# Two halves to a block: pv and scores of a sparse-attention kernel in three blocks per chunk, not six

## The chip, the cores and the metric

The kernel runs on one core of a Trainium2 chip. The metric is the device time of one execution in microseconds (us). Three runs of the kernel before took 757.9, 758.04 and 759.26 us; the median is 758.04.

## What is computed

The input has 4 batches, 8 heads, 768 positions and 64 columns per head, all in 32-bit floats. A block-sparse attention is followed by a two-layer net with a squared relu:

```python
scores = scale * np.matmul(q, k.transpose(0, 1, 3, 2))
mask = np.abs(blk_i - blk_j) <= window            # blocks of 32, window 1
mask |= first and last block, as a query or as a key
mask[...] = True                                  # 3 sampled blocks per block of queries
scores = np.where(mask, scores, -1000000000.0)
attn = exp(scores - max); attn /= sum + 1e-09
x = (attn @ v)  as 3072 tokens x 512
h = np.maximum(x @ w_in, 0.0)                     # 512 x 2048
return h * h @ w_out                              # 2048 x 512
```

(Lines of the reference, shortened; `attn`, `x` and the mask's second line stand for several lines each.)

## The kernel before

**Tiles and chunks.** A batch has six tiles of 128 queries (four blocks of 32). Three tiles make a chunk of 384 tokens, so that there are 24 tiles in 8 chunks, and an even chunk begins a batch. A tile's work is done in two halves of four heads each (class `Half`). A block of 32 queries has 256 keys at its place: the first and the last block, three sampled and three of the window.

**The MoE of a chunk** (`moe`, `hidden`, `project`) is a loop over 16 slices f of the hidden layer. `turn` transposes the chunk's three tiles (xt, L773). Then for each f come `project(f - 2)`, nine matmuls into three accumulators (po, L826), and `hidden(f)`, twelve matmuls into one bank (ph, L788). To keep the precision, each operand is split into a high and a low part: ACT makes r and gh from ph (L792, L799), DVE makes gf (L804) and the casts wi and wo (L754), POOL makes the low parts gl (L806), wi and wo (L755). The results of a chunk are stored when the next one has begun.

**The attention of chunk c + 1 runs inside the MoE of chunk c.** The MoE's generators stop after every 3 or 4 matmuls; one such stop is a piece, 96 to a chunk, six to a slice f. `Stream.step` is called at each piece, first goes on with the units that have begun, then starts new ones, and each unit says by `yield n` how many pieces later it wants to go on. The engines take their instructions in the order in which they are written here. So the table `LAG`, `STEP` (16 pieces from one half to the next), `EARLY` and `G_AT` set the order on every engine.

**A half from the seventh tile on** (`MOVED`): scores `s` are 64 small matmuls from kn (the batch's keys, window) and KG (gathered keys) into two PSUM banks (L374). DVE takes maxima (L385) and subtracts them (L391), which frees the banks. ACT takes 16 exps of 32 rows each, which also move blocks (pm, L413). DVE turns pm into pT (L418). PE then makes pv, 64 small matmuls from pT and V (L459), and DVE divides (`norm`, L474 to L479). With the table's numbers pv of one half falls on the piece at which the scores of a later one begin: a block of pv and s, six per chunk. The first six tiles go another way (exps with a bias, transposes pt on PE).

**The first and last block of queries** of a batch see all keys. These are `Whole` units, one per pair of heads, four per batch, in even chunks: scores g (L546), maxima, exps into pg, 32 copies of 32 rows into pgm (L571, by ACT and POOL in turns), a transpose by DVE (L577), and pvg (L604), which needs vn, the batch's values in two halves. One buffer holds vn: its second half is loaded when pvg of the second pair has read the first.

**Buffers and loads.** Five PSUM banks are handed out in turn to ph, xt, s, g, pv and pvg; three more hold the accumulators po. V has one buffer for each half of the heads, KG has two tiles, kn one buffer per half. SP issues nearly all loads, in the written order: after pv of a half the V rows of the next tile (one or two window loads L304, a read of the sampled indices L231, twelve sampled loads L317); with the scores of a tile's second half q (L242) and the gathered keys of the tile after next (L276, twelve); at a batch's last tile kn, QG and vn of the next batch (L175, L170, L222). The KG slots for the first and last block of keys are copied from kn by ACT (`next_keys`, `static_keys`, L284), for tiles 0 and 1 of batches 1 to 3.

Of the kernel before, what the change touches and what calls it, by code (L numbers as in the profile page):

```python
# [10 lines left out]
F32 = mybir.dt.float32  # L11
# [61 lines left out]
LAG_1 = {**LAG, "v": 10, "x": 3, "t": 6, "v0": 5, "n": 0}  # L73
LAG_0 = {"s": 2, "x": 2, "t": 3, "c": 2, "v0": 2, "n": 2}

CUT_0 = (30, 5)
# [20 lines left out]
def tile_block_sparse_attention_moe(ctx: ExitStack, tc, kd, knd, qd, qgd, vd, vnd, samp, const, wcat, out):  # L97
# [182 lines left out]
    def static_keys(b, t, u, copy=nc.scalar.copy):  # L280

        src = st["kn", b, u][:, 0 : NBLK : NBLK - 1].rearrange("p i a c -> p i (a c)").unsqueeze(1)
        dst = st["kg", b, t][:, :, 0:2, 2 * u : 2 * u + 2].rearrange("p j i a c -> p j i (a c)")
        copy(dst, src.broadcast_to(list(dst.shape)))  # L284
# [39 lines left out]
    class Half:  # L324
# [8 lines left out]
        def run(self, bank, lag):  # L333

            self.scores()
            self.loads(0)
            yield lag["s"]
            self.maxima()
            if self.moved:
                yield lag["e"]  # L340
                yield from self.turn_blocks()
                yield lag["v"]
            else:
                yield lag["x"]
                self.exps()
                self.next_keys()
                yield lag["t"]
                pt = self.turn(bank)
                yield lag["c"]
                self.copies(pt)  # L350
                self.loads(1)
                yield lag["v0"]
            po = self.values(bank)
            if lag["n"] >= 0:
                yield lag["n"]
            self.norm(po)
            self.loads(2)
# [37 lines left out]
                    op=ALU.subtract,  # L395
                )

        def next_keys(self):

            b, t = order[min(self.k + self.u, len(order) - 1)]  # L400
            if b > 0 and t < 2:
                static_keys(b, t, 1 - self.u)

        def turn_blocks(self):


            x = self.p.rearrange("p h c a s -> p (h c) a s")
            p = rot.tile([P, NJ, 8, BLK], F32, tag="p", name=f"pm{self.name}", bufs=PBUFS)
            for j in range(NJ):
                if j == 2:  # L410
                    self.next_keys()
                for a in range(NJ):
                    nc.scalar.activation(  # L413
                        p[a * BLK : (a + 1) * BLK, j], x[j * BLK : (j + 1) * BLK, :, a], AF.Exp, scale=SCALE
                    )
                    yield 1
            self.pT = rot.tile([P, NJ, 4, 2, BLK], F32, tag="pT", name=f"pT{self.name}", bufs=2)
            nc.vector.transpose(self.pT.rearrange("p j h c q -> p (j h c q)"), p.rearrange("p j x s -> p (j x s)"))  # L418

        def exps(self):  # L420
            for e in range(2):
# [59 lines left out]
        def loads(self, step):  # L481
# [19 lines left out]
            if step == 2 and k not in range(1, UC) and n < len(order):  # L501
# [2 lines left out]
                load_window(n, self.u)  # L504
                load_sampled(n, self.u, nc.sync, SP)

    class Whole:


        n = (16 * BLK, 8 * BLK)  # L510

        def __init__(self, b, pr):
            self.b, self.pr = b, pr
            self.name = f"{b}_{pr}"

        def run(self, bank, lag):
            self.scores()
            yield lag["s"]
            self.maxima()
            yield lag["x"]  # L520
            self.exps()
            yield lag["t"]
            if self.b > 0:
                yield from self.move()
                yield lag["w0"]
                self.turn_blocks()
                yield lag["w"]
# [36 lines left out]
        def move(self):  # L564

            self.pm = rot.tile([P, NJ, NT, BLK], F32, tag="w", name=f"pgm{self.name}", bufs=WBUFS)
            x = self.p.rearrange("p (k a s) -> p k a s", k=NT, a=NJ)
            for g in range(NJ):
                for a in range(NJ):
                    copy = nc.scalar.copy if a % 2 else nc.gpsimd.tensor_copy  # L570
                    copy(self.pm[a * BLK : (a + 1) * BLK, g], x[g * BLK : (g + 1) * BLK, :, a])  # L571
                    if a % 2:
                        yield 0

        def turn_blocks(self):
            self.pT = rot.tile([P, S], F32, tag="pT", name=f"pTg{self.name}", bufs=2)
            nc.vector.transpose(self.pT.rearrange("p (k g q) -> p g k q", k=NT, g=NJ), self.pm)  # L577

        def turn(self, bank):
            pt = [bank(f"ptg{self.name}_{i}") for i in range(2)]  # L580
# [4 lines left out]
            return pt  # L585

        def copies(self, pt):
            self.pT = rot.tile([P, S], F32, tag="pT", name=f"pTg{self.name}", bufs=2)
            for i, n in enumerate(self.n):
                at = i * self.n[0]  # L590
                if i == 0:
                    nc.scalar.copy(self.pT[:, at : at + n], pt[i][:, :n])
                else:
                    nc.vector.tensor_copy(self.pT[:, at : at + n], pt[i][:, :n])

        def values(self, bank):
            b, pr = self.b, self.pr
            vn = st["vn", b, pr // 2]
            po = bank(f"pvg{self.name}")
            for kt in range(NT):  # L600
                a = kt * P
                for g in range(4):
                    h = pr % 2 * 2 + g % 2
                    nc.tensor.matmul(  # L604
                        po[g * BLK : (g + 1) * BLK, :VW],
                        self.pT[:, a + g * BLK : a + (g + 1) * BLK],
                        vn[:, kt, h * VW : (h + 1) * VW],
                        start=(kt == 0),
                        stop=(kt == NT - 1),
                    )  # L610
            return po
# [16 lines left out]

    def units(c):

        halves = [Half(b, t, u) for b, t in order[c * UC : (c + 1) * UC] for u in range(2)]
        wholes = [] if c % 2 else [Whole(c // 2, pr) for pr in range(NPAIR)]
        if c == 0:
            return [(i * STEP_0, u) for i, u in enumerate(wholes + halves)]
        if c == 1:
# [377 lines left out]
```

## Time and profile before

| | |
|---|---|
| times of the runs | 757.9, 758.04, 759.26 us |
| profiled execution, span from first to last instruction | 757.7 us |
| its time beside the span | not recorded apart; the fastest run shown is 0.2 us over the span |
| PE busy | 733.0 us (97%) |
| weight loads on PE | 612.4 us (81%) |
| ACT, POOL, DVE busy | 539.4, 502.1, 500.2 us |
| granted TensorE clock, mean | 0.993 |

| turn of chunk (first xt) | at us | to the next |
|---|---|---|
| 0 | 57.51 | 98.7 |
| 1 | 156.18 | 92.1 |
| 2 | 248.28 | 83.9 |
| 3 | 332.18 | 92.5 |
| 4 | 424.69 | 83.9 |
| 5 | 508.60 | 91.8 |
| 6 | 600.41 | 80.3 |
| 7 | 680.74 | 77.0 to the end |

The stretch that starts with the turn of an odd chunk holds the attention of an even one, with its four `Whole` units, which is why these are longer. In the profile a line such as "PE L788 MATMUL ph<-xh,WI ... x12" is twelve matmuls written at line 788 of the kernel that put xh and WI into ph. [...] SPq is SP's queue, where a DMA row is its issue; "us to landing" is the time from there until the data is in.

### The profile page before, as it was taken

What the parts mean: (1) busy time and instruction counts of PE and PEld (TensorE: products, weight loads), DVE (VectorE), ACT (ScalarE), POOL (GpSimd) and SP (SyncE); (2) the same over time, 40 slices, a digit from 0 to 9 for tenths busy, and PEclk for the clock granted to TensorE, in tenths of its full rate; (3) what the DMA queues carried; (4) which work ended last, traced back from release to release, by engine and by line L of the source; (5) the groups of instructions that cost most, each with busy time, mean ns of one, the idle gap of its engine ahead of it and who ended that gap; (6) DMA issues with size and microseconds to landing.
All of it is one profiled execution on the core that took longest, in us unless ns stands there. A gap on an engine that the chain in (4) does not pass through costs nothing.

```text
span 757.7 us, 26295 instructions
## 1 busy us (share of the span) xinstructions
PE 733.0 (97%) x9832; PEld 612.4 (81%) x9832; DVE 500.2 (66%) x988; ACT 539.4 (71%) x1193; POOL 502.1 (66%) x636
## 2 busy tenths in 40 slices
PE   5779999999999999999999999999999999999997
PEld 2666777678888888888888888887888888888986
DVE  5785785658785756667777575666868666645452
ACT  5896877898876876689786767679876776733222
POOL 6963844237776675757777567666876575777885
PEclk9899999999999999999999999999999999999999
DMA  8776799644443436544434344654344352201001
GB/s 282 217 210 187 223 272 339 136 119 141 125 119 92 144 90 186 153 105 118 119 102 107 98 126 107 225 120 139 84 122 114 81 138 65 51 1 44 1 1 42
DMA packets 92434, 97.45 MB, mean 129 GB/s; under 512 B 14803, under 2 KB 79700, under 8 KB 92308
## 3 DMA queue, kind: packets, MB, share of 16 engines
q1 hardware_dynamic: 86324, 72.80, 36.6%
q0 software_dynamic: 5696, 22.58, 8.8%
q8 instruction: 78, 1.28, 0.7%
q14 instruction: 48, 0.39, 0.2%
q10 hardware_dynamic: 288, 0.39, 0.1%
HBM read 89.43 MB, written 6.29 MB: 126 GB/s over the span
## 4 chain that ended last, share of the span: by engine, by line
PE 84%; DMA 5%; ACT 5%; DVE 3%; issue 1%; SPq 1%; POOL 1%; ACTq 0%; POOLq 0%; DVEq 0%
PE ph L788 33%; PE po L826 30%; PE s L374 7%; PE pv L459 6%; DMA V<-in_v_dram 3%; PE po L816 3%; PE g L546 2%; PE pvg L604 2%; DMA KG<-in_k_dram 1%; PE pt L437 1%; PE xt L773 1%; DVE xl L777 1%; ACT V L209 1%; DMA kn<-in_kn_dram 1%; SPq L317 1%
## 5 line engine op out<-in xcount | busy, mean ns | idle before, releaser
L413 ACT ACTIVATE pm<-p 32x256 f32<-32x256 f32 x576 | 239.2, 415 | 13.2 <-DVE p L391 4.9
L788 PE MATMUL ph<-xh,wi 128*128 128x384 f32 x832 | 237.8, 347 | 0.0
L826 PE MATMUL po<-wo,gh 128*128 128x512 f32 x672 | 213.8, 399 | 0.0
L755 POOL TENSOR_TENSOR wi<-W,wi 128x512 fp32r<-128x512 f32 x104 | 142.2, 1367 | 66.8 <-DVE wi L754 35.2
L806 POOL TENSOR_TENSOR gl<-gf,gh 128x384 fp32r<-128x384 f32 x112 | 117.4, 1048 | 93.3 <-DVE gf L804 80.9
L755 POOL TENSOR_TENSOR wo<-WO,wo 128x512 fp32r<-128x512 f32 x112 | 145.8, 1301 | 49.5 <-DVE wo L754 48.6
L792 ACT ACTIVATE r<-ph 128x384 f32<-128x384 f32 x128 | 63.0, 492 | 161.6 <-PE ph L788 156.5
L804 DVE SCALAR_TENSOR_TENSOR gf<-ph,r 128x384 f32<-128x384 f32 x112 | 62.3, 556 | 150.7 <-ACT r L792 137.1
L788 PEld LDWEIGHTS ph<-xh,wi 128*128 128x128 f32 x832 | 150.4, 188 | 13.4 <-issue 7.4
L826 PEld LDWEIGHTS po<-wo,gh 128*128 128x128 f32 x672 | 123.5, 188 | 23.0 <-issue 2.8
L788 PE MATMUL ph<-xl,wi 128*128 128x384 f32 x416 | 141.4, 340 | 0.0
L826 PE MATMUL po<-wo,gl 128*128 128x512 f32 x336 | 133.1, 396 | 0.0
L754 DVE CAST wo<-WO 128x512 fp32r<-128x512 f32 x112 | 84.3, 753 | 0.0
L788 PEld LDWEIGHTS ph<-xl,wi 128*128 128x128 f32 x416 | 78.2, 188 | 6.9 <-issue 2.9
L826 PEld LDWEIGHTS po<-wo,gl 128*128 128x128 f32 x336 | 63.1, 188 | 15.7 <-POOL gl L806 1.0
L385 DVE TENSOR_REDUCE m<-s 128x2 f32<-128x512 f32 x96 | 61.6, 683 | 10.6 <-PE s L374 10.2
L799 ACT ACTIVATE gh<-r 128x384 fp32r<-128x384 f32 x112 | 59.0, 527 | 9.3 <-ACT r L792 0.4
L459 PEld LDWEIGHTS pv<-V,pT 128*32 128x32 f32 x3072 | 47.2, 109 | 18.9 <-issue 10.5
L459 PE MATMUL pv<-V,pT 128*32 128x65 f32 x3072 | 56.0, 221 | 4.4 <-ACT pT L446 2.3
L788 PE MATMUL ph<-xh,WI 128*128 128x384 f32 x192 | 54.4, 344 | 0.8 <-ACT xh L776 0.8
L374 PE MATMUL s<-KG,q 64*32 64x160 f32 x1536 | 51.3, 307 | 0.6 <-issue 0.3
L418 DVE STREAM_TRANSPOSE pT<-pm 128x1024 f32<-128x1024 f32 x36 | 44.6, 1238 | 4.9 <-ACT pm L413 4.7
(89 smaller groups left out, 933.9 us busy)
## 6 DMA issues: line engine op xcount, KB each, us to landing
craw<-in_w_dram POOLq DMA_DIRECT2D x32, 512.0 KB, 6.0
V<-in_v_dram SPq DMA_DIRECT2D x504, 32.5 KB, 1.8
KG<-in_k_dram SPq DMA_DIRECT2D x216, 64.0 KB, 2.0
V<-in_v_dram SPq DMA_DIRECT2D x28, 390.0 KB, 4.3
q<-in_q_dram SPq DMA_DIRECT2D x24, 256.0 KB, 3.6
out_dram<-ot SPq DMA_DIRECT2D x22, 256.0 KB, 2.6
V<-in_v_dram SPq DMA_DIRECT2D x16, 292.5 KB, 4.0
vn<-in_vn_dram SPq DMA_DIRECT2D x5, 780.0 KB, 6.2
```

The costliest lines, as they stand in the source:

```text
L374: nc.tensor.matmul(self.sb[e][j * BLK : (j + 1) * BLK, i * NSLOT + a : i * NSLOT + z], q[r, j, pr, :], k, start=True, stop=True,)
L385: nc.vector.tensor_reduce(m[:, e], self.sb[e].rearrange("p (i c) -> p i c", i=2), axis=AX, op=ALU.max)
L413: nc.scalar.activation(p[a * BLK : (a + 1) * BLK, j], x[j * BLK : (j + 1) * BLK, :, a], AF.Exp, scale=SCALE)
L459: nc.tensor.matmul(po[j * BLK : (j + 1) * BLK, h * VW : (h + 1) * VW], self.pT[:, j, 2 * e + i, c], v[:, self.u, j, hv : hv + VW], start=( ...
L754: nc.vector.tensor_copy(w[:, 0], src)
L755: nc.gpsimd.tensor_tensor(w[:, 1], src, w[:, 0], op=ALU.subtract)
L788: nc.tensor.matmul(ph[:, :TOK], w, x, start=(i == 0), stop=(i == len(steps) - 1))
L792: nc.scalar.activation(r, ph[:, :TOK], AF.Relu)
L799: nc.scalar.activation(gh, r, AF.Square)
L804: nc.vector.scalar_tensor_tensor(gf, ph[:, :TOK], 0.0, r, op0=ALU.max, op1=ALU.mult)
L806: nc.gpsimd.tensor_tensor(gl, gf, gh, op=ALU.subtract)
L826: nc.tensor.matmul(acc[c][u], g[:, at], w[:, k], start=(f == 0 and i == 0), stop=(f == NF - 1 and i == 2))
```

## The change

Instead of two `Half` units a tile from the seventh on is one `Pair`. It writes the scores of both halves together, then maxima and subtractions of both (one piece later), then 32 exps spread evenly over a window of pieces (pieces in the table `CROWDED` count for three quarters), each half's transpose one piece behind its exps, the KG copies three pieces and one piece ahead of the next block, and at the end pv of both halves, after which both divide and load. Blocks begin at pieces 0, 35 and 66 of 96 (`BLOCKS`). The `Whole` units get their own places: g at 3, 18, 38 and 74, pvg at 35, 47, 66 and 96 (`WHOLES`). Of pgm's copies ACT's half goes to DVE, and its transpose is cut in two, into buffers of another tag (ct). The first six tiles, the MoE and what is computed stay.

```diff
-STEP = PIECES // (2 * UC)
-EARLY = 23
+EARLY = 9
-LAG = {"s": 0, "e": 4, "v": 11, "x": 4, "t": 4, "c": 0, "v0": 13, "w0": 4, "w": 16, "n": -1}
-G_AT = 9
+BLOCKS = (0, 35, 66)
+SECOND = 1
+TURN = 1
+BUSY = 0.75
+CROWDED = (*range(PIECES - 3, PIECES), *range(14))
+WINDOWS = ((5, 31), (6, 27), (4, 25))
+BEFORE = 4
+KEYS_AT = 3
+LAG = {"s": 0, "x": 4, "t": 4, "w0": 4, "n": -1}
+WHOLES = ((3, 35), (18, 47), (38, 66), (74, 96))
...
+    class Pair:
+        def __init__(self, b, t, at, plan):
+            self.halves = [Half(b, t, u) for u in range(2)]
...
+        def events(self):
+            first, second = self.halves
+            ends, begin, end = self.plan
+            ev = [(1, first.maxima), (SECOND, second.maxima), (ends - KEYS_AT, lambda: first.next_keys(0))]
+            ev.append((ends - KEYS_AT + 2, lambda: first.next_keys(1)))
+            weight = [BUSY if (self.chunk + n) % PIECES in CROWDED else 1.0 for n in range(begin, end)]
...
+        def run(self, bank, lag):
+            if self.first:
+                static_keys(self.b, self.t, 1)
+                yield BEFORE
+            for h in self.halves:
+                h.scores()
+                h.loads(0)
+            now = 0
+            for at, do in self.events():
+                if at > now:
+                    yield at - now
+                    now = at
+                do()
+            yield self.plan[0] - now
+            po = [h.values(bank) for h in self.halves]
+            for h, x in zip(self.halves, po):
+                h.norm(x)
+                h.loads(2)
...
-                    copy = nc.scalar.copy if a % 2 else nc.gpsimd.tensor_copy
+                    copy = nc.vector.tensor_copy if a % 2 else nc.gpsimd.tensor_copy
...
-            self.pT = rot.tile([P, S], F32, tag="pT", name=f"pTg{self.name}", bufs=2)
-            nc.vector.transpose(self.pT.rearrange("p (k g q) -> p g k q", k=NT, g=NJ), self.pm)
+            self.pT = [rot.tile([P, S // 2], F32, tag="ct", name=f"pTg{self.name}_{i}", bufs=2) for i in range(2)]
+            for i in range(2):
+                nc.vector.transpose(
...
-        both = [(at + i * STEP, u) for i, u in enumerate(halves)]
-        both += [(at + i * STEP + G_AT, u) for i, u in enumerate(wholes)]
+        both = []
+        for i, x in enumerate(BLOCKS):
+            ends = (*BLOCKS[1:], PIECES)[i] - x
+            u = Pair(*tiles[i], (x - EARLY) % PIECES, (ends, *WINDOWS[i]))
+            both.append((at + x - (BEFORE if u.first else 0), u))
+        if c % 2 == 0:
+            turned = 1 + 1 + LAG["x"] + LAG["t"] + 2 * NJ + LAG["w0"]
+            both += [(at + x, Whole(c // 2, pr, y - x - turned)) for pr, (x, y) in enumerate(WHOLES)]
```

**PE, around pvg of the third pair, chunk 4** (pvg_2 reads vn_1, the second half of vn). Before:

```order
L826 MATMUL po_0_6697<-wo_7_7325,gl_7_7356 128x512
L604 MATMUL pvg_2_7413<-vn_1_7148,pTg_2_7157 32x65 x24
L826 MATMUL po_1_6698<-wo_7_7325,gh_7_7352 128x512 x2
L826 MATMUL po_1_6698<-wo_7_7325,gl_7_7356 128x512
L826 MATMUL po_2_6699<-wo_7_7325,gh_7_7352 128x512 x2
L826 MATMUL po_2_6699<-wo_7_7325,gl_7_7356 128x512
```

And with the change:

```order
L887 MATMUL po_1_6567<-wo_7_7190,gl_7_7215 128x512
L659 MATMUL pvg_2_7275<-vn_1_7108,pTg_2_0_7230 32x65 x12
L659 MATMUL pvg_2_7275<-vn_1_7108,pTg_2_1_7231 32x65 x12
L887 MATMUL po_2_6568<-wo_7_7190,gh_7_7211 128x512 x2
L887 MATMUL po_2_6568<-wo_7_7190,gl_7_7215 128x512
L463 MATMUL pv_1_0_7310<-V_78,pT_1_0_7164 32x65 x4
```

In PE's order pvg of the third pair stands in the same slice (between the po runs of f = 7) as before, one run of three po later. On SP the rows around the load of vn_1 are the same as before (V, V, q, twelve gathered keys, vn); before, the two groups of V loads wait for the pv of two blocks, now for the two pv of one.

**SP, at the change of batch in chunk 3** (kn_0, kn_1: keys of the next batch; V_79, V_78: V rows). Before:

```order
L175 DMA kn_0_5572<-in_kn_dram 128x1536
L170 DMA QG<-in_qg_dram 128x512
L222 DMA vn_0_5575<-in_vn_dram 128x1560
L304 DMA V_79<-in_v_dram 96x3x260
L304 DMA V_79<-in_v_dram 96x260
L231 TENSOR_LOAD idx
...
L317 DMA V_79<-in_v_dram 32x260
L175 DMA kn_1_5805<-in_kn_dram 128x1536
```

And with the change:

```order
L324 DMA V_79<-in_v_dram 32x260
L182 DMA kn_0_5755<-in_kn_dram 128x1536
L177 DMA QG<-in_qg_dram 128x512
L229 DMA vn_0_5758<-in_vn_dram 128x1560
L182 DMA kn_1_5794<-in_kn_dram 128x1536
L249 DMA q_1_5796<-in_q_dram 128x512
```

kn_1 stood behind the next V loads, one block later; now it follows vn_0, and the V loads of both halves stand ahead of kn_0.

**ACT, the copies of the new batch's keys into KG, same place.** Before and with the change:

```order
L284 COPY KG_94<-kn_0_5572 128x4x2x64
L413 ACTIVATE pm_5_1_5891<-p_5_1_5858 32x256 x2
L792 ACTIVATE r_11_5958<-ph_11_5942 128x384
...
L413 ACTIVATE pm_0_0_6127<-p_0_0_6092 32x256 x2
L284 COPY KG_94<-kn_1_5805 128x4x2x64
```

```order
L860 ACTIVATE gh_13_6047<-r_13_6045 128x384
L291 COPY KG_94<-kn_0_5755 128x4x2x64
L291 COPY KG_94<-kn_1_5794 128x4x2x64
L853 ACTIVATE r_14_6356<-ph_14_6331 128x384
```

The second copy stood among the exps of the next tile's first half (pm_0_0); now it stands ahead of r of slice 14, behind the first copy.

More of the change, by code (lines that the diff above doesn't have):

```diff
@@ L338, in run @@
             self.maxima()
[L339 to L352, printed above, removed]
+            yield lag["x"]
+            self.exps()
+            if self.u == 1:
+                self.next_keys(0)
+            yield lag["t"]
+            pt = self.turn(bank)
+            yield lag["c"]
+            self.copies(pt)
+            self.loads(1)
+            yield lag["v0"]
             po = self.values(bank)
@@ L526, in run @@
                 self.turn_blocks()
-                yield lag["w"]
+                yield self.wait
             else:
@@ L587, in copies @@
         def copies(self, pt):
-            self.pT = rot.tile([P, S], F32, tag="pT", name=f"pTg{self.name}", bufs=2)
+            pT = rot.tile([P, S], F32, tag="pT", name=f"pTg{self.name}", bufs=2)
             for i, n in enumerate(self.n):
@@ L591, in copies @@
                 if i == 0:
-                    nc.scalar.copy(self.pT[:, at : at + n], pt[i][:, :n])
+                    nc.scalar.copy(pT[:, at : at + n], pt[i][:, :n])
                 else:
-                    nc.vector.tensor_copy(self.pT[:, at : at + n], pt[i][:, :n])
+                    nc.vector.tensor_copy(pT[:, at : at + n], pt[i][:, :n])
+            self.pT = [pT[:, i * S // 2 : (i + 1) * S // 2] for i in range(2)]
         def values(self, bank):
@@ L600, in values @@
             for kt in range(NT):
-                a = kt * P
+                i, a = divmod(kt * P, S // 2)
                 for g in range(4):
```

55 lines of the change are left out of this document (36 added, 19 removed).

## The prediction

> **What bounds the kernel now.** I read the page's busy times first, then the chain of waits, then the timeline of PE.
>
> ```profile
> PE 733.0 (97%) x9832; PEld 612.4 (81%) x9832; DVE 500.2 (66%) x988; ACT 539.4 (71%) x1193; POOL 502.1 (66%) x636
> ```
>
> Busy PE is no proof, since matmul ends are modelled. The chain of waits (start, length, engine, name, line, count) is better: around a block it holds nothing but PE.
>
> ```profile
> 430.37 2.11 PE ph L788 x12
> 432.48 1.05 PE pv L459 x64
> 433.53 1.14 PE s L374 x63
> 434.67 2.29 PE ph L788 x12
> 436.95 2.10 PE po L826 x9
> 439.05 2.08 PE ph L788 x12
> ```
>
> So TensorE's own stream sets the end in chunks 1 to 6, and time changes in two ways only: the stream gets shorter, or something makes PE wait. A hidden step f of the MoE costs 2.08 + 2.10 = 4.18 us, that is six pieces of 0.70. The ph run behind a block takes 2.29 instead of 2.08.
>
> **What the change removes: switches.** PE's timeline (start, duration, engine, line, what, shape, count):
>
> ```profile
> 432.14 0.34 PE L788 MATMUL ph<-xh,WI 128*128 128x384 f32 x1
> 432.41 1.12 PE L459 MATMUL pv<-V,pT 128*32 128x65 f32 x64
> 433.46 0.40 PE L374 MATMUL s<-kn,q 64*32 64x96 f32 x16
> ...
> 433.92 0.37 PE L374 MATMUL s<-kn,q 64*32 64x96 f32 x16
> ...
> 434.60 0.45 PE L788 MATMUL ph<-xh,wi 128*128 128x384 f32 x1
> 434.89 0.33 PE L788 MATMUL ph<-xl,wi 128*128 128x384 f32 x1
> ```
>
> Starts count here, not durations. A ph matmul starts every 2.08/12 = 0.17 us, so after 432.14 the next was due at 432.31; pv starts at 432.41: 0.10 to enter. The two halves of s start 0.46 apart, so s would be through at 434.38, but ph starts at 434.60 (0.22), and its second at 0.29 instead of 0.17 (0.12): 0.34 to leave. For the step from pv to s I compare with a run of 48 of the same shape:
>
> ```profile
> 401.57 0.89 PE L604 MATMUL pvg<-vn,pTg 128*32 128x65 f32 x48
> 402.39 0.62 PE L788 MATMUL ph<-xh,wi 128*128 128x384 f32 x2
> ```
>
> 48 take 0.82 and 64 take 1.05, so 16 cost 0.23, 64 cost 0.92, and 0.13 is paid once per run. A block removed is worth 0.10 + 0.13 + 0.34 = 0.57 us.
>
> How many: between one turn (xt) and the next there are six blocks now and three afterwards, five times: 15. In the sixth such stretch two more go: 17 x 0.57 = 9.7. The last two pv runs join (0.3), two lone s runs in chunk 1 join (0.10 + 0.34 = 0.4), and pvg of the fourth pair moves in between pv and s in three chunks (3 x 0.23 = 0.7). Together 11.1 us. The bounds are 8 (runs of one shape also pay 0.13 where the half changes, 18 x 0.17) and 12.
>
> A second gain: chunks 2, 4 and 6 have g ahead of a block, and s then waits for a bank that ACT's exp of g still reads.
>
> ```profile
> 342.58 0.70 ACT pg L562
> ...
> 343.32 1.19 PE s L374 x55
> ...
> 519.00 0.70 ACT pg L562
> ```
>
> Those two s runs last 2.24 instead of 1.14 from the end of pv to ph, 1.1 us each. In the new order at least five other banks are handed out between any g and the next scores, so 2.2 us go. Bounds 0 and 3.
>
> **What it adds: the queue of SP.** Each tile's V rows, q and gathered keys are issued by SP, one behind the other. V of both halves is now free only in the one block, so SP runs V, V, q, KG in one stretch behind it, and the load of vn's second half (needed by pvg of the third pair) stands behind all that, though it may go as soon as pvg of the second pair is done. The kernel before has the same stretch once per two chunks:
>
> ```profile
> 358.13 1.22 PE L459 MATMUL pv<-V,pT 128*32 128x65 f32 x64
> ```
>
> ```profile
> 347.18 0.41 SPq L304 DMA_DIRECT2D V<-in_v_dram  x1
> 349.31 6.33 SPq L317 DMA_DIRECT2D V<-in_v_dram  x12
> 359.39 0.34 SPq L304 DMA_DIRECT2D V<-in_v_dram  x1
> 360.71 6.97 SPq L317 DMA_DIRECT2D V<-in_v_dram  x12
> 367.77 0.37 SPq L242 DMA_DIRECT2D q<-in_q_dram  x1
> 369.13 7.02 SPq L276 DMA_DIRECT2D KG<-in_k_dram  x12
> 376.25 0.38 SPq L222 DMA_DIRECT2D vn<-in_vn_dram  x1
> ```
>
> ```profile
> 177.06 0.41 SPq L304 DMA_DIRECT2D V<-in_v_dram  x1
> ...
> 204.45 0.36 SPq L222 DMA_DIRECT2D vn<-in_vn_dram  x1
> ```
>
> ```profile
> vn<-in_vn_dram SPq DMA_DIRECT2D x1, 780.0 KB, 5.0
> ```
>
> From the first V to vn are 29.07 us; 3.65 of it (355.64 to 359.39, less 0.1) is SP waiting for the pv at 358.13, which leaves 25.4. The same stretch at 177.06 has no such gap: 27.4. V goes out 1.26 us after its pv starts, and vn lands 5.0 after its issue. So vn is there 1.26 + 25.4 + 5.0 = 31.7 us after the block's first pv (33.7 in the slower case).
>
> When does PE come to pvg of the third pair? The merged block takes 2 x 0.92 + 0.13 + 2 x 0.92 + 0.34 = 4.15. From there to pvg stand one third of a po run, then ph and po by turns up to two thirds of the po run behind ph 8: five ph and five po runs, 20.9. Besides one g, and one pvg (0.82 + 0.10):
>
> ```profile
> 495.32 1.29 PE g L546 x4
> ```
>
> 4.15 + 20.9 + 1.29 + 0.92 = 27.3. PE waits 4.4 us, up to 6.4, in each of chunks 2, 4 and 6: three times 4.4 is 13.2. The low bound takes the shortest pieces: with 1.3 from a window to its twelve, 6.3 for V and 6.1 for KG the stretch is 22.9, vn lands at 28.9, the wait is 1.6. So 5 to 19 us, and I take 13.2, from the commoner stretch.
>
> At a change of batch the same happens to the natural keys. Before, kn of each half was issued one block apart; now V, V, kn, QG, vn, kn go out in a row, and ACT's copy into KG, then s of the second half, need the last of them.
>
> ```profile
> 287.02 0.88 SPq L304 DMA_DIRECT2D V<-in_v_dram  x2
> ...
> 295.37 0.36 SPq L175 DMA_DIRECT2D kn<-in_kn_dram  x1
> ```
>
> ```profile
> vn<-in_vn_dram SPq DMA_DIRECT2D x1, 780.0 KB, 7.3
> ```
>
> ```profile
> kn<-in_kn_dram SPq DMA_DIRECT2D x1, 768.0 KB, 4.7
> ```
>
> ```profile
> L284 ACT COPY KG<-kn 128x512 f32<-128x512 f32 x12 | 7.5, 625 | 0.2
> ```
>
> V with two windows takes 8.35, twice 16.7, so the first kn is issued at 18.0. kn, QG and vn together were in 0.88 + 7.3 = 8.2 after kn's issue, a lone kn 4.7 after it: 1036 KB in 3.5, so a fourth transfer of 768 KB adds 2.6 and lands at 28.8. The copy ends at 29.5. PE comes to that s after 4.15 + 5 x 4.18 = 25.1 and 0.10 + 1.97 + 0.92 in the block: 28.1. It waits 1.4 us, bounds 0 and 3, twice (batches 2 and 3; batch 1 is loaded by POOL): 2.8.
>
> **What I cost at nothing.** DVE's maxima and subtractions now come for two halves in a row:
>
> ```profile
> L385 DVE TENSOR_REDUCE m<-s 128x2 f32<-128x512 f32 x96 | 61.6, 683 | 10.6 <-PE s L374 10.2
> L391 DVE TENSOR_TENSOR p<-s,m 128x512 f32<-128x512 f32 x72 | 46.0, 680 | 0.1
> L571 ACT COPY pgm<-pg 32x192 f32<-32x192 f32 x96 | 33.6, 350 | 1.5
> ```
>
> Four of each are 5.5 us instead of 2.7, and gf, wo and wi queue behind them; what PE needs of those is used two steps f (8.4 us) later, which covers it, and if not, the excess is paid per block. The exps are spread over 21 to 26 pieces, and the 96 copies of pgm (0.35 us each) leave ACT for DVE, which has room in the page's sum (66%); they cost PE nothing unless DVE falls behind.
>
> **Sum.** The profiled execution spans 757.7 us, the runs shown have a median of 758.0, 0.3 more. 757.7 - 11.1 - 2.2 + 13.2 + 2.8 = 760.4, with the 0.3 **761 us**.
>
> **Rivals.** *SP is in time.* If vn and kn land before PE comes, only the gain is left: 757.7 - 13.3 + 0.3 = 745; with the low bounds (3 x 1.6, kn 0) 750. For it: SP's twelves vary (6.33 and 6.97 above) and may come out shorter in the new order. Against: it needs a stretch of 27.3 - 1.3 - 5.0 = 21 us from V to vn, and the shortest pieces give 22.9.
>
> *DVE becomes the bound in chunks 2, 4 and 6.* Its casts show what meeting POOL costs:
>
> ```profile
> L754 DVE CAST wo<-WO x112: 382/428/1549, 164.5 to 746.3; 128x512 fp32r<-128x512 f32 x112
> 157.00:248.00 91.00, 91.00 (x1307) 75.57 (x1306) 66.24 (x138) 72.44 (x170) 60.52 (x67) 1.00 0.46 119
> ```
>
> Median 0.43 us, longest 1.55. DVE is busy 66.2 of 91 us in such a chunk (the third busy time). 32 copies of 0.35 make 77; if each is held up by 0.4 they make 90, against a PE stream of 91 - 3. From about 0.3 of delay per copy DVE decides, and PE waits some 3 us per chunk more: 770. [...]
>
> *The switches do not pay.* If the 0.57 belongs to the halves and not to the blocks, the gain is 2.2 alone: 772. The run of 48 speaks against it.
>
> **Chances.** Forecast 0.5, own range 754 to 767; SP in time 0.3 (743 to 752); DVE 0.13; switches 0.07. This measurement tells about 0.2%, 1.5 us, from no change: below 756.5 is faster, above 759.6 slower. Of the forecast's half 0.11 lies below and 0.14 between; with the first rival faster has 0.41, the same 0.14, slower 0.45. The range 744 to 769 leaves out the best of the first rival and the last two in part.
>
> **What would show it.** Right: the timeline shows pvg of the third pair starting 3 to 6 us behind its po run in chunks 2, 4 and 6, released by the landing of vn, and s of the second half waiting for ACT's KG copy before a new batch; three blocks of about 4.15 us between turns; no s released by ACT's pg. Wrong: pvg of the third pair follows po at 0.1 us (then SP was in time), or PE's waits for gl or wi from POOL and DVE grow past 3 us per chunk.

## The result and the profile after

The changed kernel takes 800.8 us (median of four runs, 798.5 to 803.7) against 758.65 for the kernel before beside it: a ratio of 1.054, 95% interval 1.051 to 1.058. It is slower, as forecast, but by 42 us and not by 3; the time lies far outside the range.

| from turn to turn (first xt) | before, us | after, us | difference |
|---|---|---|---|
| 1 (with g) | 92.1 | 101.3 | +9.2 |
| 2 | 83.9 | 90.4 | +6.5 |
| 3 (with g) | 92.5 | 100.8 | +8.3 |
| 4 | 83.9 | 89.0 | +5.0 |
| 5 (with g) | 91.8 | 102.3 | +10.4 |
| 6 | 80.3 | 82.3 | +2.0 |

Every stretch with merged blocks is longer. The busy times and, below them, the chain's shares (two rows of the page):

```profile
PE 736.4 (92%) x9832; PEld 618.9 (78%) x9832; DVE 566.1 (71%) x1096; ACT 501.2 (63%) x1097; POOL 503.9 (63%) x636
...
PE 72%; DVE 9%; ACT 7%; DMA 5%; issue 5%; POOL 1%; SPq 0%; ACTq 0%; POOLq 0%; DVEq 0%
```

PE's work is the same (9832 matmuls), its share fell from 97% to 92%, and "issue" has 5% of the chain. PE waits now. Rows from the list of waits of the changed kernel (us in total, times, longest; PEld is the weight loads, whose rows show the same waits):

```profile
PEld s L377 <- issue: 30.4, 28, 2.8
PE s L377 <- issue: 21.5, 16, 2.5
PEld po L887 <- POOL gl L867: 12.8, 13, 2.2
PE po L887 <- POOL gl L867: 7.5, 10, 1.8
PE pv L463 <- DVE pT L420: 3.3, 3, 1.1
PE pvg L659 <- DMA vn<-in_vn_dram: 0.5, 1, 0.5
```

and the rows that answer to the third and the second in the kernel before:

```profile
PEld po L826 <- POOL gl L806: 1.0, 4, 0.3
PE s L374 <- issue: 0.3, 1, 0.3
```

The wait that carried the prediction, pvg for vn, is there once, with 0.5 us. In its place stand two that the sum did not have: s waits for nothing that the profile shows ("issue"), and po waits for gl.

**The first new wait: PE runs out of instructions.** The timeline of one merged block:

```profile
209.44 1.55 PE L463 MATMUL pv<-V,pT 128*32 128x65 f32 x86
211.50 0.87 PE L463 MATMUL pv<-V,pT 128*32 128x65 f32 x42 [0.50 <-issue]
212.30 0.40 PE L377 MATMUL s<-kn,q 64*32 64x96 f32 x16
...
213.44 0.43 PE L377 MATMUL s<-KG,q 64*32 64x160 f32 x4
215.71 0.35 PE L377 MATMUL s<-KG,q 64*32 64x160 f32 x6 [1.85 <-issue]
...
216.64 0.45 PE L849 MATMUL ph<-xh,wi 128*128 128x384 f32 x1
```

The block takes 7.2 us instead of 4.15: PE stops in the middle of pv and again in the middle of s, where the profile shows nothing that it waits for. The page lists a queue of instructions:

```profile
q8 instruction: 78, 1.28, 0.7%
```

78 packets of 16 KB, for 20,103 records of PE in the trace (9832 matmuls, as many weight loads, 439 of its sequencer): 258 to a packet in the mean, and I count with 256. A block before had 128 matmuls with their 128 weight loads, 256 instructions in 2.2 us, and the next came 11 us later. A merged block has 512, which were to take 4.15 us. No two packets start less than 3.6 us apart in this trace. From the first turn on there are 21 gaps of more than 0.8 us inside pv or s, from one start to the next; 16 of them end for no reason that the profile shows. I set these against the packets (start of the gap, its length, how long before PE went on the last packet had landed, and how many of PE's records, weight loads and semaphores included, stand between the last multiple of 256 and the gap; the first and the last of 16 and four between them):

```
gap at    length   packet landed before PE went on   records behind a multiple of 256
180.70    0.87     1.34                              193
213.57    2.14     1.36                              193
331.79    2.79     1.35                              193
497.01    2.77     1.48                              193
595.89    2.72     1.45                              193
687.04    1.16     1.63                              193
```

All 16 end 1.1 to 1.6 us after a packet has landed; together they are 25.8 us, about one gap to a block. And all 16 stand at the same count, 193 (the count begins at the profile's first record, so the border need not be at 0): I take that place for the border of two packets. The other five gaps wait for DVE (three for pT, two for a bank that DVE's division reads) and stand at other counts. In all 17 traces of this case, 113 gaps of this length inside pv, s or pvg stand at the 193, every one put down to issue; of the 80 gaps elsewhere 79 are put down to another engine or a DMA. The kernel before has two gaps of that length, the waits for g's bank, which end 8.7 and 14.7 us after a packet.

The same count gives an estimate of how far ahead PE was supplied. I pair packets and borders in their order, with the smallest shift at which every packet has landed before PE passes its border. Then, from the first turn on, a packet in every trace started only when PE was at most 298 instructions short of its border, and PE never passed that border sooner than 1.1 us after the landing. So by this pairing PE had little more than one packet ahead of it when the next one started. Where PE stopped in the changed kernel, it took 3.1 to 5.0 us from one border to the next, while a block of the kernel before runs its 256 small instructions in 2.2: a merged block's 512, two packets' worth, starved.

The longest stop cost more than itself. The chain at it, and the windows around it (the column behind the engines is the granted clock):

```profile
331.01 1.07 PE s L377 x57
332.08 2.50 issue
334.58 2.17 PE s L377 x62
336.75 3.04 PE ph L849 x12
```

```profile
324.80:332.00 7.20, 7.20 (x206) 6.19 (x204) 5.62 (x13) 5.08 (x12) 5.81 (x5) 1.00 1.01 388
332.00:334.50 2.50, 0.08 (x3) 0.00 (x0) 0.49 (x1) 0.13 (x1) 1.46 (x2) 1.00 0.34 89
334.50:336.70 2.20, 2.12 (x72) 1.63 (x72) 1.60 (x3) 0.00 (x0) 0.00 (x0) 0.60 0.41 113
336.75:339.80 3.05, 3.05 (x14) 3.05 (x14) 3.05 (x6) 0.00 (x0) 0.00 (x0) 0.74 0.79 207
```

After 2.5 us of idling the granted clock was 0.60 in the mean of 2.2 us and 0.74 in the 3.05 us behind them; the rest of s took twice its time and the ph run 3.04 instead of 2.10: 2 us more. It does not follow every long stop: behind the other two of this length, at 497 and 596 us, the clock stayed at 1.00. Between 150 and 790 us the clock of the changed kernel stands at 0.50 three times, for 3.4 us each, and that of the kernel before never; this is at most 5 of the 42 us.

**The second new wait: DVE falls behind in the stretches with g.** Windows of the changed kernel, turn to turn, with g, without and with (busy PE, PEld, DVE, ACT, POOL):

```profile
153.40:254.70 101.30, 92.86 (x1316) 77.29 (x1315) 83.11 (x174) 62.05 (x141) 63.20 (x75) 1.00 0.41 108
254.70:345.10 90.40, 85.70 (x1122) 75.32 (x1120) 59.28 (x101) 60.18 (x137) 56.10 (x46) 0.98 0.44 125
345.10:445.90 100.80, 93.30 (x1322) 79.63 (x1321) 84.57 (x175) 62.01 (x141) 64.92 (x77) 0.98 0.41 106
```

DVE is busy 83 to 85 us there (67 to 68 of 92 before), and the new copies are dearer than the 0.35 us they had on ACT:

```profile
L621 DVE COPY pgm<-pg x96: 247/364/1370, 157.7 to 622.8; 32x192 f32<-32x192 f32 x96
```

Their mean is 0.59 us; 30 of the 96 take over 0.6, up to 1.37, about one POOL instruction (gl 1.06, wo 1.30) more than the shortest. In the trace each of these 30 runs beside a POOL instruction and ends 0.11 to 0.12 us behind its end; the 13 with no POOL instruction beside them took 0.25 to 0.26.

### The profile page after: what moved, and what is told of

Its sections match the earlier page's. It is cut to its first block, busy times and chain, and to the rows that moved or that the text cites. A ratio compares the mean times of both kernels' runs of the same rounds, so it can differ in the third digit from the quotient of the medians.

```text
span 796.7 us, 26360 instructions
## 1 busy us (share of the span) xinstructions
PE 736.4 (92%) x9832; PEld 618.9 (78%) x9832; DVE 566.1 (71%) x1096; ACT 501.2 (63%) x1097; POOL 503.9 (63%) x636
## 4 chain that ended last, share of the span: by engine, by line
PE 72%; DVE 9%; ACT 7%; DMA 5%; issue 5%; POOL 1%; SPq 0%; ACTq 0%; POOLq 0%; DVEq 0%
PE ph L849 28%; PE po L887 25%; PE s L377 6%; PE pv L463 5%; PE po L877 3%; DMA V<-in_v_dram 3%; DVE pgm L621 3%; PE g L596 2%; DVE wi L815 1%; PE pvg L659 1%; DVE pT L420 1%; ACT pm L413 1%; DMA KG<-in_k_dram 1%; ACT p L427 1%; ACT pT L450 1%
## 5 line engine op out<-in xcount | busy, mean ns | idle before, releaser
L849 PEld LDWEIGHTS ph<-xh,wi 128*128 128x128 f32 x832 | 152.9, 189 | 9.5 <-issue 4.9
L887 PE MATMUL po<-wo,gl 128*128 128x512 f32 x336 | 134.8, 401 | 7.5 <-POOL gl L867 7.5
L815 DVE CAST wo<-WO 128x512 fp32r<-128x512 f32 x112 | 89.1, 796 | 0.5
L463 PEld LDWEIGHTS pv<-V,pT 128*32 128x32 f32 x3072 | 51.1, 109 | 22.6 <-issue 11.3
L463 PE MATMUL pv<-V,pT 128*32 128x65 f32 x3072 | 58.0, 221 | 10.9 <-ACT pT L450 5.0
L377 PE MATMUL s<-KG,q 64*32 64x160 f32 x1536 | 53.1, 310 | 14.3 <-issue 14.3
L621 DVE COPY pgm<-pg 32x192 f32<-32x192 f32 x96 | 56.6, 590 | 1.9
```

The lines of the kernel that those rows point to most:

```text
L377: nc.tensor.matmul(self.sb[e][j * BLK : (j + 1) * BLK, i * NSLOT + a : i * NSLOT + z], q[r, j, pr, :], k, start=True, stop=True,)
L463: nc.tensor.matmul(po[j * BLK : (j + 1) * BLK, h * VW : (h + 1) * VW], self.pT[:, j, 2 * e + i, c], v[:, self.u, j, hv : hv + VW], start=( ...
L815: nc.vector.tensor_copy(w[:, 0], src)
L849: nc.tensor.matmul(ph[:, :TOK], w, x, start=(i == 0), stop=(i == len(steps) - 1))
L887: nc.tensor.matmul(acc[c][u], g[:, at], w[:, k], start=(f == 0 and i == 0), stop=(f == NF - 1 and i == 2))
```

## The experiments

Two theories. **I**: PE's instructions come too slowly for a long block. **D**: DVE's copies, held up by POOL, make gl and pT late. Rivals: the crowding of ACT's windows (W), and that a long block stalls for some other reason.

**1. The copies back on ACT (copies_on_act).**

```diff
-copy = nc.vector.tensor_copy if a % 2 else nc.gpsimd.tensor_copy
+copy = nc.scalar.copy if a % 2 else nc.gpsimd.tensor_copy
```

> The changed kernel with one of its parts undone: the 96 copies of pgm that went to DVE are on ACT again, as before. Theory D (DVE falls behind in the chunks with g: in the profile of the changed kernel the copies average 590 ns, and po waits for gl 12.8 + 7.5 us): those waits go, and with them 14 to 20 us: 781 to 787. If DVE were the whole loss, 758 to 765. Theory I (PE's instructions come too slowly for the long blocks: 'issue' waits of s 21.5 us): nothing of that changes, and if I were the whole loss, 798 to 802. I expect both causes, so 784, with the issue waits of s still above 18 us.

809.0 us (ratio to the kernel before 1.063, interval 1.060 to 1.066): 8 us slower, not faster. The waits of s for issue stayed (22.2 us), and po now waits for ACT's gh too (6.2 us, none before). ACT seems to have no room in the new order: 32 exps of 0.415 us in windows of 21 to 26 pieces of 0.7. My expectation took it that a copy taken from DVE comes free elsewhere.

**2. The blocks cut in two (split4, split4_act).** Scores start four pieces behind pv, with a ph and some po between; two g move by four pieces.

```diff
+GAP = 4
-WHOLES = ((3, 35), (18, 47), (38, 66), (74, 96))
+WHOLES = ((7, 35), (18, 47), (42, 66), (74, 96))
+            yield GAP            # ahead of the scores of a Pair
```

> The changed kernel with its blocks cut in two: scores of the next tile start four pieces (2.8 us) after pv of both halves, with ph and po between; the two g that would stand right ahead of a score run start four pieces later as well, the copies of pgm stay on DVE. Theory I: 512 instructions of PE in 4 us are more than the fetches of 256, which never start less than 3.6 us apart in the trace, can supply; 256, then 2.8 us with 30 to 40, then 256 can be supplied. The issue waits of s (21.5 us) fall below 4, pv's too: minus 22 to 27; the 17 or 18 cuts cost 0.44 each for entering and leaving, 8 in all: 800.8 - 25 + 8 = 784, 779 to 790. If the loss were DVE's or the queue of SP's, the cuts cost 8 and bring nothing: 805 to 810.

> Both: blocks cut in two by four pieces, and the copies of pgm on ACT. Theories I and D together: the gains add, 800.8 - 17 - 17 = 767, 760 to 775, and what stands above the kernel before should then be the wait of pvg of the third pair for vn that the prediction had (4.4 us in each of three chunks). If vn comes in time after all, it should be near 755. If the loss is one thing that either edit cures, the two together bring no more than the better one alone.

824.9 us (1.084, 1.082 to 1.087) and 843.7 (1.109, 1.104 to 1.113): slower again. But the gaps at the packets' borders are gone, all of them: what is left over 0.8 us in pv or s is six waits for pT between the halves and three of s for a bank that DVE's division reads, and in stretch 2 s takes 5.7 us from start to start of its matmuls, as before the change (5.5), not 11.5. What came in its place is told by the chain of split4 between 275 and 345 us:

```profile
by line: ACT pm L414 39.9%; PE ph L852 15.6%; PE po L890 8.8%; PE s L378 7.2%; DVE pT L421 7.2%; issue 6.4%; PE pv L464 6.3%; ACT r L856 4.8%; ACT gh L863 4.1%; ACTq L863 0.2%
```

My edit began the exps four pieces later and ended them where they ended, so ACT sets the time. The run shows that cutting cures the gaps; it says nothing of the gain.

**3. Cut the other way round (sfirst4, sfirst4_act).** Scores four pieces ahead of pv, so that the exps keep their window; the loads stay behind pv.

```diff
-EARLY = 9
+EARLY = 13
+GAP = 4
-            yield self.plan[0] - now
+            yield self.plan[0] + GAP - now
```

> The changed kernel with its blocks cut the other way round: scores of the next tile four pieces (2.8 us) ahead of pv, so that the window of the exps is as long as in the changed kernel; the loads stay behind pv, the copies of pgm on DVE. In split4 the waits inside the scores went (5.7 us from score to score between two turns instead of 11.5), but the exps had four pieces less, and PE waited for ACT (chain: ACT pm 21%). Theory I + W (instructions come too slowly for a long block; split4's new loss is ACT's shortened window): the score gaps go and nothing takes their place: 800.8 - 5 x 5.7 + 18 x 0.44 = 780, 775 to 786. Rival (cutting the block costs as such, whichever way): as split4, 815 to 830. What is left above the kernel before in the stretches with g is then the part of DVE and ACT.

> As sfirst4, with the copies of pgm back on ACT. In copies_on_act this cost 8 us instead of gaining: ACT, with 32 exps of 0.415 us in 21 to 26 pieces of 0.7, has no room for them. Theory W (ACT's window is full in the changed order): it costs 5 to 12 here too, 785 to 792. Theory D (DVE's copies are a loss and ACT was only late because PE had starved): it gains 5 to 15 here, 765 to 775.

823.0 us (1.080, 1.076 to 1.085) and 809.6 (1.064, 1.060 to 1.069). The expectation failed for other waits: at two changes of batch s comes four pieces earlier and finds kn not landed (gaps of 2.6 and 2.9 us at 334 and 339, 2.0 and 2.6 at 533 and 536), and pvg of the fourth pair waits 2.4 us for pTg from DVE in each of three stretches (7.1 in all). Scores four pieces earlier put DVE's maxima and subtractions, 5.5 us, ahead of that transpose. A second way of cutting thus meets two other waits that were just covered. With the copies on ACT this order is 13 us faster, where the changed kernel became 8 us slower: which engine has room for them depends on the order. Part of these times is the clock: between 150 us and the end it stands at 0.50 for 37.5 us in sfirst4, 20.5 in sfirst4_act and 47.8 in split4_act, against 10.2 in the changed kernel.

**4. The dose, in the old order (old_s_thrice, old_s_x3).** The kernel before, with each score run three times as long: 512 instructions to a block. First with each matmul repeated in place:

```diff
+for _ in range(3 if self.moved else 1):
     nc.tensor.matmul(...)
```

> The kernel before, in its own order, with each score matmul from the seventh tile on issued three times into the same place (the result is the same): 36 blocks of 512 PE instructions instead of 256, all else as it was. The added work by itself is 36 x 2 x 0.92 = 66 us: 758 + 66 = 824 if PE is limited by its matmuls alone. Theory I: each block now asks for 512 instructions in 4.1 us and starves for 1.5 to 2 us as the merged ones do: 36 x 1.7 = 60 more, 870 to 895, with issue waits of s above 40 us.

1024 us, with no issue waits: a miss of the experiment. A matmul repeated in place took 0.044 us from start to start instead of 0.014 and never asked for instructions fast. So the loop went around the whole run:

> The kernel before in its own order, with the whole score run of each half issued three times over from the seventh tile on (the result is the same). The run old_s_thrice issued each matmul three times in a row, which by itself made one take 0.05 us instead of 0.014, so it never asked for instructions fast; here the order within a run is as it was. PE limited by its matmuls: 36 x 2 x 0.92 = 66 more, 822 to 828, no issue waits. Theory I: 512 instructions in a row as in a merged block, another 1.5 to 2 us of issue waits in each of 36 blocks: 870 to 895. An order of before, so neither ACT, DVE nor SP is later than PE.

904.7 us (1.187, 1.181 to 1.193): 66 us are the added matmuls by the expectation's estimate, 78 more are not, 2.2 per block. The waits:

```profile
PEld s L375 <- issue: 67.5, 49, 3.9
PE s L375 <- issue: 55.1, 35, 3.6
```

Of 36 gaps over 0.8 us inside the blocks, 35 end 1.2 to 1.7 us after a packet of instructions has landed, all 35 at the count of 193. The order of the work on ACT, DVE and SP is that of the kernel before: theory I stands by itself. Of the 23 by which the 78 is over 55 I put 19 down to the clock, an estimate: between 150 and 900 us it stands at 0.50 ten times behind a stop (570 to 573 us, for one), 37.5 us in all, which is 19 us of full speed; four other stops of 2 us or more were not followed by it.

**5. One part alone, in the old order (old_dve_copies).** The kernel before with the odd copies of pgm on DVE.

> The kernel before with one part of the change alone: the 96 odd copies of pgm on DVE instead of ACT, the order and the blocks as they were. Theory D (these copies on DVE make po wait for gl and wo, whatever the order): the three stretches with g become 3 to 4 us longer, 767 to 771. Theory W (it is the new order that crowds DVE and ACT; in the old order there is room for the copies on either engine): 756 to 761.

760.3 us against 761.0 (0.998, 0.995 to 1.000): the copies cost nothing there. Its copies are shorter:

```profile
L571 DVE COPY pgm<-pg x96: 250/256/1367, 156.0 to 564.6; 32x192 f32<-32x192 f32 x96
```

12 of 96 are over 0.6 us instead of 30. It is the new order that makes them dear: D needs both.

**6. What DVE's copies cost in the new order (no_dve_copies, reduce_copies).** Once they are left out and the transposes read pg itself (so the whole heads' sums are not right); once they are written as reductions:

```diff
-copy(self.pm[a * BLK : (a + 1) * BLK, g], x[g * BLK : (g + 1) * BLK, :, a])
+nc.vector.tensor_reduce(self.pm[a * BLK : (a + 1) * BLK, g],
+    x[g * BLK : (g + 1) * BLK, :, a].unsqueeze(3), axis=AX, op=ALU.max)   # odd a
```

> The changed kernel with the 96 copies of pgm on DVE left out (the transposes read pg itself, so the four whole heads' sums come out of places that are not theirs; POOL's 96 copies still run): what did they cost in this order, given that on ACT they cost 8 us more and in the old order nothing on DVE? Theory D2 (in the new order DVE is full in the stretches with g, 83 to 85 us busy of 101, so po waits for gl and pv for pT because of these copies): of the 3 to 3.5 us from po to po and the 2 to 3 us from pv to pv that each of the three stretches has more than before, most goes: minus 12 to 18, 783 to 789. Theory W (the shortened windows of the exps are the cause, DVE's copies only a part): minus 0 to 5, 796 to 801. In both the issue waits of s stay.

> The changed kernel with DVE's 96 copies of pgm written as a maximum over an axis of one element, which moves the same data. In the changed kernel 30 of these 96 copies took over 0.6 us, up to 1.37, the others 0.25 to 0.36. Theory L (a copy on DVE is held by POOL's instructions for their length, a reduction is not): the mean falls from 590 ns to below 420 with hardly any above 0.7, and the po waits for gl with it: minus 4 to 12, 789 to 796. If the mean stays, copies are late for another reason: 799 to 803. [...]

792.3 us (1.041, 1.038 to 1.045) and 795.0 (1.048, 1.044 to 1.052), 8.5 and 5.8 under the changed kernel: between the two theories of the first expectation, within that of the second. The interval of the second one's ratio overlaps that of the changed kernel (1.051 to 1.058) a little, so the 5.8 is not sure by itself. The reductions of reduce_copies:

```profile
L621 DVE TENSOR_REDUCE pgm<-pg x96: 337/345/350, 158.8 to 617.9; 32x192 f32<-32x192 f32 x96
```

No single one is held up: 0.34 to 0.35 us each, where the copies took 0.25 to 1.37. And a wait comes out from behind the others:

```profile
PE pvg L663 <- DMA vn<-in_vn_dram: 4.6, 3, 2.6
```

**7. Longer windows (wide).** `WINDOWS = ((5, 33), (5, 29), (4, 28))` instead of ((5, 31), (6, 27), (4, 25)).

> The changed kernel with wider windows for the exps: 28, 24 and 24 pieces instead of 26, 21 and 21, all else as it was. 32 exps of 0.415 us are 13.3 us; 21 pieces of 0.7 are 14.7 us, in which ACT also has r and gh of three to four steps. Theory W (ACT too full in its windows makes gh, gf and then gl late): minus 4 to 10, 791 to 797. Theory D2 (DVE is what is late): no gain, 799 to 803. If pT, which comes after the last exp, has no time left, pv waits instead: 803 to 812.

810.3 us (1.065, 1.062 to 1.069): the last of its three cases. pv waits for pT 13.8 us. Theory W as a cause of the slowdown by itself finds nothing here: in the new order an exp that ends later makes pT late; that one that ends earlier crowds ACT is likely from split4's chain, and not tested by itself. Only 6 gaps of instructions are left (13.4 us); that a block which stops for pT gives the packets time to come is my reading, not tested.

**8. One term alone (old_g7).** The kernel before with `G_AT = 7` instead of 9.

> The kernel before with g two pieces earlier (at piece 7 of 16 instead of 9), so that ACT's exp of g is through before the next scores ask for its bank. It tests one term of the prediction, the 2.2 us that the changed order was to save by itself: if those waits were worth that, ratio 0.997, and the trace shows no score waiting for ACT's pg; if another wait takes their place, 1.000.

758.55 against 759.9 us (0.998, 0.996 to 1.000), and no score waits for ACT's pg any more; s waits 1.1 us for ACT's KG instead and xt 1.5 for DVE's gf. The waits were real and can be moved away; whether the time was, 1.3 us of the 2.2 at an interval that ends at no change, stays open.

**9. Half the instructions, the same columns (old_half_instr, half_instr, half_instr_reduce).** The decisive test: order and columns stay, but pv and s need half as many instructions. Which keys and heads the columns belong to is no longer right, so the result is not the attention.

```diff
-for piece in range(2): ...               # s: 96 columns of kn, 160 of KG
+k = kg[r, j, 0:2] if i == 0 else kn[r, 4 * j : 4 * j + 4]      # 256 columns
-for e in range(2): ...                   # pv: 65 columns per head
+for e in range(1): ...                   # 130 columns, two heads
```

> Control for the next two: the kernel before with half as many PE instructions in pv and s and the same number of columns moved. From the seventh tile on a score matmul moves 256 columns instead of 96 and 160 (for the first pair of heads all from KG, for the second all from kn), and a pv matmul moves 130 columns for two heads with the weights of the first; the result is no longer the attention, the rest of the kernel is as it was. A block asks for 128 PE instructions instead of 256. If the columns set PE's time, 752 to 762; if each instruction costs its start, 36 x (0.46 + 0.46) = 33 less, 725.

> The changed kernel with pv and s in half the instructions, as in the control (the same columns, a result that is not the attention): a merged block asks for 256 instructions instead of 512. Theory I: the issue waits inside the blocks (s 21.5, and 5 to 10 in pv and pvg) go, 25 to 30 us more than whatever the control gains: if the control stays at 758, 770 to 777. Then PE is early enough for the wait on vn that the prediction had, and pvg of the third pair waits for it 1 to 4 us in three stretches. If the stalls inside the blocks come from something else (a bank, the weights, the clock), the change is that of the control, 800 if it stays at 758.

> As half_instr, with DVE's copies of pgm written as reductions, which POOL doesn't hold up. Both causes gone, the changed order should show the prediction's own sum: 757.7 - 11.1 - 2.2 + 13.2 + 2.8 + 0.3 = 761 if the control stays at 758, 756 to 770, with pvg of the third pair waiting 3 to 6 us for vn in three stretches. If SP is in time there, 745 to 750 and no such wait.

The control takes 754.0 us (0.993, 0.991 to 0.995), the changed order 775.2 (1.020, 1.014 to 1.025), and with DVE's reductions 761.8 (1.003, 1.000 to 1.005). The waits of s for issue fall from 21.5 to 0.4 us. So the supply of instructions is worth 800.8 - 775.2 = 25.6, less the control's 5.0: 20.6 us; DVE's held copies are worth 13.5 once PE is fast enough, and 5.8 when it starves. The two cover each other: together they are 34 us of the 42, and half_instr_reduce stands the other 8 above its control. None of its gaps over 0.8 us stands at a packet's border. Four are in s and wait for banks, and what is left at a change of batch is the wait that the prediction had there:

```profile
319.06 2.09 PE L467 MATMUL pv<-V,pT 128*32 128x130 f32 x64
322.97 0.67 PE L380 MATMUL s<-KG,q 64*32 64x256 f32 x16 [1.81 <-ACT KG L291]
```

```profile
PE s L380 <- ACT KG L291: 3.1, 2, 1.8
```

## Why the prediction was right and wrong

**The step that failed** is the price of a merged block. The prediction worked it out from the starts of its matmuls alone ("The merged block takes 2 x 0.92 + 0.13 + 2 x 0.92 + 0.34 = 4.15") and took it, without a reason, that PE gets its instructions as fast as it can start them. In the changed kernel the 14 blocks without a pvg in them took 5.3 to 7.9 us, 6.2 in the mean; with half the instructions such a block took 3.8 where it waited for nothing. The rows of the kernel before could not show the loss, since with 256 instructions in 2.2 us and then 11 us of slack PE stopped at a border for 0.6 us at the most; they did show what to set it against. Its packets start 3.6 us apart at the least, with 256 instructions each, and one block had 0.29 us of issue wait in the middle of s. That was enough for an estimate: if two packets take no less than twice that, 7.2 us, and a block was to take 4.15, up to 3 us could be lost in each of 17 blocks; the 16 long stops come to 1.5 for each (25.8 us).

**"What I cost at nothing"** failed in part, as a second step. The copies of pgm cost PE nothing "unless DVE falls behind", and DVE did: 13.5 us with PE in step, 5.8 under the starving. The casts of wo had shown such delay in the kernel before: 48 of its 112 took over 0.6 us, each ending 0.28 to 0.29 us behind a POOL instruction, and the 31 with none beside them 0.38 to 0.42. The rival "DVE becomes the bound" had this cause, and some 9 us for it (770 against 761) where the runs show up to 13.5, and got a chance of 0.13; its own point of decision, 0.3 us of delay per copy, was nearly met by a mean of 0.59 for the copies against 0.345 for the reductions.

**The wait for vn** was right on SP's side and not on PE's. SP's rows of the changed kernel, behind the pv at 369.04:

```profile
370.22 0.36 SPq L311 DMA_DIRECT2D V<-in_v_dram  x1
...
388.71 7.41 SPq L283 DMA_DIRECT2D KG<-in_k_dram  x12
396.22 0.38 SPq L229 DMA_DIRECT2D vn<-in_vn_dram  x1
```

vn goes out 25.5 to 27.2 us behind the first pv in the three stretches (26.7 in the text). But PE came to pvg at 30.0 to 32.2, not 27.3, being late from its own stops. With DVE's held copies away pvg waited 4.6 us in all, with both causes away 0.4: there the block before it still lost 0.9 to 2.8 us in s, to banks that DVE's norm reads. The 13.2 us measured at most 4.6 in the order of the change (5.1 in sfirst4). The low bound of that wait was also mis-added: 1.26 + 22.9 + 5.0 - 27.3 is 1.9 us and not 1.6; only the low bounds hang on it (5 us here, 750 us in the first rival).

**The switches** were over-priced. Between turns 1 and 7 of the table half_instr_reduce stands 6.0 us above its control. I find 3.3 in it for the keys, 6.9 inside s in the stretches with g, 2.3 for gl and 0.7 ahead of pvg, 13.2 in all, and 2.6 for g's bank in the control, so by this estimate from one trace of each the merging itself gave about 13.2 - 2.6 - 6.0 = 4.6 us, not 11.1. Part of the reason is in the starts: where one half joins the next without a block's end between them, pv pays 0.10 and s 0.15 (half_instr_reduce over its control in stretch 4, three joins each), which the text had only as its low bound.

**Right:** the waits for g's bank (gone after the change, and in old_g7; their 2.2 us of time are not shown), and the 2.8 us for the new batch's keys (1.8 and 1.3 in half_instr_reduce; in the changed kernel the starving hides them). The sum of 761 came out in half_instr_reduce, 761.8, but by luck, as errors that cancel: 6.5 us less gain from the switches and some 13 less wait for vn, with 6.9 and 2.3 of other waits and a control that is 5 faster. It is not a confirmation.

## What to carry to other kernels

Count the instructions of a run of small matmuls, weight loads too, and set them against the packets of the instruction queue: here about 256 to a packet, and packets no less than 3.6 us apart. The short bursts of the kernel before, with large matmuls between them, hid this (the longest stop at a border, from the first turn on, is 0.6 us), and merging two of them into one that is over a packet turned saved switches (some 0.3 us each) into stops of 0.9 to 2.8 us. Where an engine stops for no reason that the profile shows, count its instructions: here all 16 such stops stood at one place in 256, and in half_instr_reduce none was left. When a move frees one engine, ask what the other one meets: the same copy on DVE took 0.25 us with POOL idle, and up to 1.37 beside a POOL instruction. And where two waits cover each other, undoing one tells little; only the pair showed what each was worth.

## What had not been expected of the hardware

The packets of PE's instructions, 16 KB each, started at least 3.6 us apart (3.4 in the longest bursts of old_s_x3), and by my pairing a packet started only when PE was at most 298 instructions short of it; where PE stopped for one, it went on 1.1 to 1.7 us after the landing. After one of three stops of some 2.5 us the granted clock stood at 0.50 for 3.4 us, after the other two not. The same small matmul issued three times in a row into one place took 0.044 us each, against 0.014 in the usual order, which takes two halves of the rows and four places by turns. Why no packet started sooner no run shows, nor which stops lower the clock, nor whether another placing of the blocks against the packets' borders would starve less.
